# Pooled attention into a gated feed-forward layer on one core: sums spread over the gaps, two value blocks in gaps of their own, six buffers for normalised blocks

## Chip, cores, metric

One NeuronCore of a Trainium2 chip. The metric is the device time of one execution in microseconds (us). A run also reports its span (first to last instruction, usually some 2 us less than the time) and the mean granted TensorE clock (1.0 is full speed). Executions over 1.5% above the fastest of their kernel are marked slow, and the ratios below leave them out.

## The reference, cut to what matters

```python
# attention: q, k, v are (8 batches, 8 heads, 576 rows, 64)
k_p = k.reshape(B, H, 72, 8, D).mean(axis=3)        # keys pooled by 8
v_p = v.reshape(B, H, 72, 8, D).mean(axis=3)        # values pooled by 8
attn = softmax(q @ k_p.T / sqrt(D)) @ v_p
x = attn.transpose(0, 2, 1, 3).reshape(4608, 512)
# feed-forward: w_gate, w_val (512, 1536), w_out (1536, 512)
out = (maximum(x @ w_gate, 0) * (x @ w_val)) @ w_out
```

## The kernel before

Tokens are worked in nine chunks of 512, numbered from 0. In chunk c TensorE (PE) does twelve *pairs* (gate and value matmuls of 128 columns of the hidden layer, eight matmuls of 512 columns) and, from chunk 2 on, seven *products* of the chunk before. A product replaces part of the output matmul by a Strassen-like scheme, which needs four *sums* of blocks of h. VectorE (DVE) forms them, each in two halves, so a chunk has eight half sums; where a run speaks of a "sum", it is one of these. Attention of batch c+1 is woven into chunk c: the key transposes, sixteen score matmul groups, and five value blocks.

```python
relu_pool = tile_pool(name="relup", bufs=3)
piece_pool = tile_pool(name="piecep", bufs=4)                # px: one normalised value block
ps_mm = tile_pool(name="ps_mm", bufs=4, space=PSUM)          # pairs, transposes
ps_at = tile_pool(name="ps_at", bufs=3, space=PSUM)          # scores, value blocks
ps_acc = tile_pool(name="ps_acc", bufs=1, space=PSUM)        # products
# ... cut ...
def values(b, t):                                            # one value block, cut
    x = piece_pool.tile([P, NG, 2, D], F16, name="px")
    for half in range(2):
        ps = ps_at.tile([P, 512], F32, name="at_ps", tag="at_ps")
        # four matmuls into ps, then on VectorE:
        nc.vector.reciprocal(out=rd[:n, half], in_=pv[:, :, D:D + 2])          # prd
        nc.vector.tensor_tensor(out=x[...], in0=pv..., in1=rd..., op=ALU.mult) # px
# back(b, t, nc.sync) then sends px through a transposing DMA into x_T
# ... cut ...
for c in range(1, n_chunks):
    # ... cut: units = pairs with products between them ...
    others, later = attention(c + 1)       # one list per gap: [keys], [], scores, values
    for i, piece in enumerate(left):       # two value blocks left over from batch 2
        others[1 + i].insert(0, piece)
    for i, unit in enumerate(units):
        if i == 3: prep(c + 2, ...)        # GpSimd pools keys and values, starts loads
        unit()
        if c == 1: run(sums[i:i + 1])
        elif i:    run(sums[2 * i - 2:2 * i])
        if i < len(others): run(others[i])
```

In the traces DVE works through its instructions in the order of this program, so the place of a sum in the loop is its place in DVE's queue. *px* is a value block after normalising (a reciprocal, *prd*, and a multiplication); until DVE has read a block out of its bank of `ps_at`, PE can't use that bank again.

The softmax here doesn't subtract the row's maximum and nothing guards it: scores larger than these inputs give would overflow.

## Time and profile before

| | value |
|---|---|
| time, three runs | 334.33, 334.46, 334.75 us |
| the execution that was profiled | 337.71 us, span 335.8, mean clock 0.990 |
| busy: PE, DVE, GpSimd (POOL), ScalarE (ACT) | 97%, 64%, 42%, 38% of the span |
| chain that ended last | PE 90%, DVE 5% |

In the profile's rows of slices a digit is the busy share (or the clock) in tenths. In a chain row the columns are start, length, engine and line. In a timeline row a bracket at the end names how long the engine stood before the instruction, and for what.

### The profile page before, as it was taken

The page shows a single profiled execution, that of the slowest core. Times are in us where ns is not written, and L with a number is a line of the kernel's source. Part 1 is how long each engine was busy: PE and PEld are TensorE (multiplying, and loading weights), DVE is VectorE, ACT ScalarE, POOL GpSimd, SP SyncE. Part 2 cuts the span into 40 slices and gives each one's busy share as a digit, 9 for nine tenths or more (in the row PEclk, how much of TensorE's full clock was granted, in tenths as well). Part 3 has the DMA queues.
Part 4 walks back from the last instruction along what each step waited for, and adds up shares of the span by engine and source line. Part 5 has one row for each costly group of instructions (what it writes and reads, how often), then busy time and mean ns, then how long its engine had stood idle before and what let it go on. Part 6 is the DMA issues. An engine that isn't in the chain of part 4 may idle for free.

```text
span 335.8 us, 6528 instructions
## 1 busy us (share of the span) xinstructions
PE 325.3 (97%) x2526; PEld 214.2 (64%) x2526; DVE 214.7 (64%) x456; ACT 128.7 (38%) x295; POOL 139.8 (42%) x186
## 2 busy tenths in 40 slices
PE   8899999999969999999999999999999999999995
PEld 2578875455536665766898966655666556566574
DVE  7465637768666757785777667766576464464562
ACT  1544562473426224722471247124822332232231
POOL 8557419999999801993099309300000000000000
PEclk9999999999969999999999999999999999999999
DMA  7999998998559246963984462243022300300224
GB/s 112 190 204 201 200 214 159 188 153 171 106 101 185 47 90 94 205 101 74 159 158 79 81 107 58 33 64 104 1 24 56 113 5 0 98 29 3 65 75 110
DMA packets 51006, 35.41 MB, mean 105 GB/s; under 512 B 30432, under 2 KB 45024, under 8 KB 50976
## 3 DMA queue, kind: packets, MB, share of 16 engines
q0 software_dynamic: 18304, 18.88, 34.3%
q1 hardware_dynamic: 32528, 16.00, 24.0%
q8 instruction: 19, 0.31, 0.4%
q10 hardware_dynamic: 144, 0.13, 0.1%
q14 instruction: 11, 0.09, 0.1%
HBM read 37.75 MB, written 9.44 MB: 141 GB/s over the span
## 4 chain that ended last, share of the span: by engine, by line
PE 90%; DVE 5%; DMA 2%; ACT 1%; issue 1%; POOL 1%; DVEq 0%; ACTq 0%; POOLq 0%
PE mm_ps L429 54%; PE acc_ps L521 19%; PE at_ps L310 5%; PE mm_ps L467 3%; PE at_ps L388 3%; PE mm_ps L594 2%; DMA q<-in_q_dram 2%; DVE px L394 1%; DVE h L438 1%; PE mm_ps L411 1%; DVE sum L512 1%; PE mm_ps L281 1%; PE mm_ps L341 1%; PE mm_ps L365 1%; ACT pexp L370 1%
## 5 line engine op out<-in xcount | busy, mean ns | idle before, releaser
L438 DVE TENSOR_TENSOR h<-mm_ps,relu 128x512 f16<-128x512 f32 (+1 forms) x120 | 76.4, 637 | 87.6 <-PE mm_ps L429 79.8
L435 ACT ACTIVATE relu<-mm_ps 128x512 f16<-128x512 f32 (+1 forms) x120 | 66.5, 554 | 137.4 <-PE mm_ps L429 135.3
L429 PE MATMUL mm_ps<-x_T,wv_sb 128*128 128x512 f16 (+1 forms) x528 | 114.0, 342 | 0.1
L429 PE MATMUL mm_ps<-x_T,wg_sb 128*128 128x512 f16 (+1 forms) x528 | 114.0, 342 | 0.0
L429 PEld LDWEIGHTS <-wv_sb 128*128 128x128 f16 x528 | 51.7, 98 | 42.9 <-issue 1.1
L429 PEld LDWEIGHTS <-wg_sb 128*128 128x128 f16 x528 | 48.7, 98 | 28.9 <-issue 1.4
L324 ACT ACTIVATE expT<-at_ps 72x288 f16<-72x288 f32 (+2 forms) x128 | 39.1, 374 | 19.0 <-PE at_ps L310 18.9
L521 PEld LDWEIGHTS <-sum 128*128 128x128 f16 x336 | 32.1, 98 | 7.2
L394 DVE TENSOR_TENSOR px<-at_ps,prd 128x256 f16<-128x256 f32 (+1 forms) x80 | 33.8, 423 | 2.7
L181 POOL TENSOR_TENSOR tree_b<-tree_a 72x256 f32<-72x256 f32 (+1 forms) x42 | 32.0, 763 | 3.3
L521 PE MATMUL acc_ps<-wo_sums,sum 128*128 128x256 f16 x252 | 31.0, 272 | 0.0
L175 POOL TENSOR_TENSOR tree_a<-v_in 72x512 f32<-72x512 f16 x24 | 29.9, 1244 | 0.1
L521 PEld LDWEIGHTS <-h 128*128 128x128 f16 x252 | 23.9, 99 | 4.1
L175 POOL TENSOR_TENSOR tree_a<-k_in 96x512 f32<-96x512 f16 x18 | 20.7, 1149 | 11.5 <-DMA k_in<-in_k_dram 11.5
L521 PE MATMUL acc_ps<-wo_sb,h 128*128 128x256 f16 x168 | 21.1, 276 | 0.0
L529 DVE TENSOR_TENSOR rows<-acc_ps,mid 128x512 f32<-128x512 f32 x21 | 14.5, 689 | 8.8 <-PE acc_ps L521 8.8
L680 POOL COPY gate<-h 128x1 f16<-128x1 f16 x4 | 1.9, 463 | 43.4 <-DVE h L438 43.4
L512 DVE TENSOR_TENSOR sum<-h 128x768 f16<-128x768 f16 x28 | 19.8, 746 | 0.1
L388 PEld LDWEIGHTS <-expT 72*128 72x128 f16 (+1 forms) x280 | 13.0, 100 | 7.5 <-DVE px L394 1.6
L393 DVE RECIPROCAL prd<-at_ps 128x4 f32<-128x4 f32 (+1 forms) x80 | 13.7, 172 | 4.0 <-PE at_ps L388 3.9
L388 PE MATMUL at_ps<-stat,expT 72*128 72x65 f16 (+1 forms) x280 | 14.8, 194 | 1.4 <-DVE px L394 1.4
L186 POOL TENSOR_TENSOR stat<-tree_b 72x128 f16<-72x128 f32 x24 | 12.1, 506 | 1.9
(106 smaller groups left out, 300.2 us busy)
## 6 DMA issues: line engine op xcount, KB each, us to landing
out_dram<-rows SPq DMA_DIRECT2D x24, 256.0 KB
k_in<-in_k_dram POOLq DMA_DIRECT2D x7, 576.0 KB, 8.0
q<-in_q_dram POOLq DMA_DIRECT2D x7, 576.0 KB, 9.9
v_in<-in_v_dram POOLq DMA_DIRECT2D x6, 576.0 KB, 13.5
wg_sb<-in_moe_w_gate_dram POOLq DMA_DIRECT2D x6, 256.0 KB, 10.9
wv_sb<-in_moe_w_val_dram POOLq DMA_DIRECT2D x6, 256.0 KB, 10.8
wo_sb<-in_moe_w_out_dram POOLq DMA_DIRECT2D x3, 512.0 KB, 9.6
v_in<-in_v_dram POOLq DMA_DIRECT2D x2, 512.0 KB, 11.3
```

What stands on the lines that cost most here:

```text
L175: eng.tensor_tensor(out=cell["a"][:n], in0=src[:, :, :4 * D], in1=src[:, :, 4 * D:], op=ALU.add)
L181: eng.tensor_tensor(out=cell["c"][:n], in0=a[:n, :, :2 * D], in1=a[:n, :, 2 * D:], op=ALU.add)
L310: nc.tensor.matmul(out=ps[:SP, c0:c0 + cnt * QP], lhsT=kpTs[b % 2][j][:, h, :], rhs=queries(b, h, i0, cnt), start=True, stop=True,)
L324: nc.scalar.activation(out=out_ap, in_=in_ap, func=AF.Exp, scale=EXP_SCALE)
L388: nc.tensor.matmul(out=ps[:n, c0:c0 + D + 1], lhsT=weights(b, h, t), rhs=stats[b % 2][:SP, g, s0:s0 + D + 1], start=True, stop=True,)
L394: nc.vector.tensor_tensor(out=x[:n, half * NG // 2:(half + 1) * NG // 2, :, :], in0=pv.rearrange("p g (x c) -> p g x c", x=2)[:, :, :, :D] ...
L429: nc.tensor.matmul(out=t[:, lo:hi], lhsT=w[:, ci, fsl], rhs=x_T[:, ci, x0:x0 + hi - lo], start=(ci == 0), stop=(ci == n_co - 1),)
L435: nc.scalar.activation(out=relu[:, :n], in_=ps[0][:, :n], func=AF.Relu)
L438: nc.vector.tensor_tensor(out=h_tiles[c][:, fo, t0:t0 + n], in0=ps[1][:, :n], in1=relu[:, :n], op=ALU.mult)
L512: nc.vector.tensor_tensor(out=S[k][:, i], in0=x[:, i], in1=y[:, i], op=op)
L521: nc.tensor.matmul(out=ps[:, tb, :], lhsT=lhs[:, i, tb * P:(tb + 1) * P], rhs=rhs[:, i, :], start=(first and tb == 0 and i == 0), stop=(tb ...
L529: nc.vector.tensor_tensor(out=out_ap, in0=x, in1=y, op=ALU.add)
```

## The change

The intent was to shorten DVE's queue at the start of a chunk, where PE waits for px, by putting one sum in each gap, and to give transposes more slack with six px buffers.

```diff
-    piece_pool = ctx.enter_context(tc.tile_pool(name="piecep", bufs=4))
+    piece_pool = ctx.enter_context(tc.tile_pool(name="piecep", bufs=6))
 ... cut: prep is split in prep_k and prep_v, both still called at unit 3 ...
+        SUMS_AT = [1, 2, 3, 4, 5, 6, 13, 14]
 ...
-                for i, piece in enumerate(left):
-                    others[1 + i].insert(0, piece)
+                if left:
+                    others[1:2] = [[piece] for piece in left]
 ...
-                elif i:
-                    run(sums[2 * i - 2:2 * i])
+                elif c == n_chunks - 1:
+                    run(sums[max(2 * i - 2, 0):2 * i])
+                elif i in SUMS_AT:
+                    sums[SUMS_AT.index(i)]()
```

## The prediction

> **What bounds the kernel now.** I read the page first. Its first part gives PE 325.3 us busy, 97% of the span, against DVE 64%, and its fourth part puts 90% of the chain that ended last on PE. So a change can only pay where PE is not fed, and the second part, in 40 slices of 8.4 us, says where that is:
>
> ```profile
> PE   8899999999969999999999999999999999999995
> ...
> PEclk9999999999969999999999999999999999999999
> ```
>
> There is one hole, slice 11 (92.3 to 100.7 us), and the granted clock falls in the same slice. To see whether anything else is left in the later chunks I took the whole chain in order of time (columns: start us, length us, engine and line, count). A chunk is 512 tokens; its twelve gate-and-value pairs are eight 512-column matmuls each (L429), 1.73 us, and three such pairs run in a row where a chunk ends and the next begins, which marks a period:
>
> ```profile
> 85.36 3.47 PE mm_ps L429 x16
> ...
> 124.10 5.18 PE mm_ps L429 x24
> ...
> 157.87 5.20 PE mm_ps L429 x32
> ...
> 225.66 5.18 PE mm_ps L429 x24
> ...
> 259.43 5.18 PE mm_ps L429 x24
> ```
>
> From 225.66 to 259.43 is 33.77 us. Its content: 12 pairs x 1.73 = 20.8, 7 output products x 1.31 = 9.2, so 30.0; the remaining 3.8 is attention work, matmuls too (24 for scores, 40 for values, 7 transposes). The next period, which has no attention, runs from 259.43 to 289.32 in the same view: 29.9 us, the sum of pairs and products to 0.1. In five windows from 131 to 299 us PE is busy for the whole of each at clock 1.00. **Chunks 3 to 7 have next to nothing to give.** Chunk 2 is different: the row at 85.36 is one pair of chunk 1 and the first of chunk 2; the same place a chunk later is 124.10 + 1.73 = 125.83. That is 40.47 us. Chunk 2 does two value blocks more than a usual chunk, 16 small matmuls; eight take 0.25 us of PE (next pair starts 0.25 after them), so 0.5. Expected 34.3, taken 40.5: **an excess of about 6.2 us**.
>
> The chain between 84 and 104 us shows what it is made of:
>
> ```profile
> 88.92 0.69 DVE h L438
> 89.61 0.66 DVE kpT1l L264
> 90.27 0.01 issue
> 90.28 0.76 DVE kpT1u L264
> 91.04 0.01 issue
> 91.06 2.31 DVE sum L512 x2
> ...
> 93.61 0.42 DVE px L394
> ...
> 96.74 3.41 PE mm_ps L429 x8
> ```
>
> DVE has become the bound for 5.7 us: two copies of pooled keys, then two sums (2.31 us together), and only then the normalising of a value block (prd, px) that frees the attention PSUM banks (three of them). PE's own timeline shows the price:
>
> ```profile
> 92.33 0.32 PE L388 MATMUL at_ps<-stat,expT 72*64 72x65 f16 x4
> 94.09 0.32 PE L388 MATMUL at_ps<-stat,expT 72*64 72x65 f16 x4 [1.45 <-DVE px L394]
> 94.64 0.31 PE L310 MATMUL at_ps<-qT,kpT1l 128*72 128x288 f16 x1 [0.23 <-DVE px L394]
> 95.45 0.40 PE L310 MATMUL at_ps<-qT,kpT1u 128*72 128x256 f16 x2 [0.49 <-ACT expT L324]
> 96.34 0.40 PE L310 MATMUL at_ps<-qT,kpT1l 128*72 128x288 f16 x1 [0.49 <-ACT expT L324]
> ```
>
> The printed ends are modelled some 0.17 us late; by the spacing of such matmuls elsewhere (4 value matmuls 0.13, a score 0.13) PE really stands for about 1.6 + 0.4 + 0.7 + 0.6 = 3.3 us. Then the clock: by stretches of 2 us it is 1.00 to 94, 0.72, 0.50, 0.50, 0.57, 1.00, which places the half clock from 94.9 to 101.7. The pair at 96.74 takes 3.41 in place of 1.73 (1.7 lost), the five score matmuls after it 0.75 for some 0.35, the next product 1.76 for 1.31: 2.5 us. Idle 3.3 + cold 2.5 = 5.8, against 6.2 from the periods. The account closes within 0.4.
>
> **The Trainium skill.** "TensorE: Matmul & The Clock Gate", Part 1, says that the array drops to half clock after a window of about 3.4 us that is not busy, and returns after a busy one. The trace agrees: 6.8 us at 0.50, two such windows. The page does not say how idle a window must be; here one with PE shown busy 1.73 of 3.41 us (91.47 to 94.88) went cold, while one at 6.14 to 9.56 with 2.62 stayed warm. "SBUF — State Buffer", Who interferes with whom, says that a DVE instruction with two SBUF inputs contends with a GpSimd instruction that reads SBUF (it says so without a figure for this pair). The sums are such: undisturbed 0.55 us (minimum 548 ns, two in 1.03 us at 165.38), but 1.15 each at 91.06, where POOL's tree_a runs beside them.
>
> **The change, part by part.** A chunk's work is laid out in 18 units (a pair or a product each); behind each unit lies a gap for attention groups and sums. (1) Chunks 2 to 7 put one sum (half of one of four) behind each of units 1 to 6, and the last two behind units 13 and 14, where two stood behind each of units 1 to 4. Same 56 instructions, none added. (2) In chunk 2 the two value blocks left over from batch 2 get gaps of their own; they push all later attention groups of that chunk one unit back, so the three scores after the second block now come behind the next pair rather than in front of it. (3) Six px buffers in place of four. (4) Splitting the pooling routine in two moves nothing: both halves are called at unit 3, and the instruction order of POOL's work stays.
>
> Working through chunk 2 with measured durations. DVE: key copies end 91.04 as before; one sum, contended, to 92.2; the four normalising instructions, shifted 1.17 us earlier, free the first bank at 92.88 and the second at 93.43. PE: pair to 92.24, first half of the second block to 92.38; its second half waits for 92.94: idle 0.5. The pair that now follows runs 93.08 to 94.81, needing nothing from DVE but copies done at 91.04. First score to 94.93. Meanwhile DVE: h 93.4 to 94.0, second sum (contended) to 95.1, block two's px at 95.75 and 96.3. The second score waits to 95.81 (idle 0.9), the third to 96.35 (idle 0.4). After that product, exps and banks are in time. **Idle 1.8 in place of 3.3; 1.5 won. If the clock stays up, another 2.5 won: 4.0.** The account left 0.4 unplaced; I give back 0.1 of it. So 334.46 - 4.1 = 330.4 us.
>
> At the other end: sums 7 and 8 now lie behind the values, before product three, which reads them at unit 16. In chunk 2, counted from unit 9 with 1.17 us of DVE per block and 0.61 for h or an add, the last sum ends 12.4 us in, and PE wants its half at 12.1 + 0.33 = 12.4: just in time. In chunk 3, rows of before (product three starts at 156.56, DVE add at 154.87) put the last sum near 156.5, in time if POOL is idle there, some 0.4 late if not. Over all six chunks 0 to 1 us lost, 0.2 expected. The px buffers: none of DVE's listed waits is for a transpose out of a px buffer, so six for four is worth 0 by itself; it gives slack only.
>
> **Rivals.** *The clock falls all the same*: 1.8 us of idle in 4 us remain, a window of 3.4 us in the worst place would be near 60% busy, between the cold and the warm window above. Then one full window at half clock costs 1.7: 332.2. For it: the window is unfavourable if it starts near 93; against: the gap is broken by a whole pair. I give it 0.3. *A new wait takes the place of the old one*: the late sums hold up product three in every chunk, 0.5 x 6 = 3 us, leaving 331.5 to 333.5. For it: slack is near zero; against: POOL is done by then in most chunks, and DVE's own timeline shows gaps of 0.2 to 1.1 us at that place of chunk 2 (119 to 126 us). Chance 0.15. *Nothing is won, since PE is 97% busy*: against it stands the excess of 6.2 us in one place. *More is won*: all 6.2 at most, 328.3; even that is 1.8%, so over 2% is nearly shut out.
>
> **Range and chances.** 0.3 x 1.8 for the clock and 0.2 for the late sums would move the mean to 331.1; the likeliest case is 330.4. I set 330.7, range 329.2 to 332.8. Faster by over 2% (under 327.8) 0.03, within 2% 0.95, slower by over 2% 0.02.
>
> **What would show it.** In the changed profile: slice 11 of PE at 8 or 9 and PEclk 9 there; in PE's timeline at 92 to 97 us three waits of 0.5, 0.9 and 0.4 for px rather than 1.45 and after; period from the first pair of chunk 2 to that of chunk 3 near 36.4 us; later periods still 33.8; first sum alone of 1.15 us before the first px. It would be wrong if a clock drop is seen in another place, if PE waits for DVE sum at L521 in the later chunks, or if a px waits for a transpose.

## The result

Six runs of the changed kernel took 333.20 to 334.41 us, median 334.14; six of the kernel before had a median of 334.78. The ratio is 0.9971 (95% interval 0.9948 to 0.9993). A ratio is the mean time of one kernel's fast runs over that of the other's of the same rounds, so not quite the ratio of the medians. So the change saves about 1 us, where 3.8 were forecast, and the time lies above the range, though within 2%, to which the prediction gave 0.95.

The slices of the changed kernel:

```profile
PE   7899999999989999999999999999999999999994
...
PEclk9999999999999999999999999999999999999999
```

Hole and half clock are gone, as hoped. The chain, for the periods:

```profile
85.74 3.45 PE mm_ps L429 x16
...
120.28 5.18 PE mm_ps L429 x24
...
154.05 5.20 PE mm_ps L429 x32
...
221.84 5.18 PE mm_ps L429 x24
...
255.61 5.18 PE mm_ps L429 x24
```

From the first pair of chunk 2 to that of chunk 3 it is 120.28 + 1.73 - 85.74 = 36.27 us, against the 36.4 that the prediction named. Later periods stay at 33.77. PE's timeline in that place:

```profile
93.49 0.31 PE L388 MATMUL at_ps<-stat,expT 72*64 72x65 f16 x4 [0.47 <-DVE px L394]
93.74 1.04 PE L429 MATMUL mm_ps<-x_T,wg_sb 128*128 128x512 f16 x4
...
95.99 0.32 PE L310 MATMUL at_ps<-qT,kpT1u 128*72 128x256 f16 x2 [0.23 <-DVE px L394]
96.53 0.31 PE L310 MATMUL at_ps<-qT,kpT1l 128*72 128x288 f16 x1 [0.22 <-DVE px L394]
```

Three stands of 0.47, 0.23 and 0.22 as printed (each some 0.17 longer by the starts, so about 0.6, 0.4 and 0.4), with the pair between the first and the second. The order and the places are those of the working; the second stand is less than half of its 0.9. Ahead of the first one DVE has one half sum now, longer than the 1.15 us forecast:

```profile
91.43 1.33 DVE L512 TENSOR_TENSOR sum<-h 128x768 f16<-128x768 f16 x1
```

Against the profile of before, the span fell from 335.8 to 332.4, by 3.4 us. **The two profiles show the gain that was forecast; the times don't.** Before against before, 337.71 against 334.46, is where the two part.

### The profile page after: what moved, and what is told of

Its sections match the earlier page's. It is cut to its first block, busy times and chain, and to the rows that moved or that the text cites. A ratio compares the mean times of both kernels' runs of the same rounds, so it can differ in the third digit from the quotient of the medians.

```text
span 332.4 us, 6528 instructions
## 1 busy us (share of the span) xinstructions
PE 322.3 (97%) x2526; PEld 212.5 (64%) x2526; DVE 210.5 (63%) x456; ACT 128.7 (39%) x295; POOL 138.8 (42%) x186
## 3 DMA queue, kind: packets, MB, share of 16 engines
q0 software_dynamic: 18304, 18.88, 34.9%
## 4 chain that ended last, share of the span: by engine, by line
PE 91%; DVE 4%; DMA 2%; issue 1%; ACT 1%; POOL 1%; DVEq 0%; ACTq 0%; POOLq 0%
PE mm_ps L429 54%; PE acc_ps L521 19%; PE at_ps L310 4%; PE mm_ps L467 3%; PE at_ps L388 3%; PE mm_ps L594 2%; DMA q<-in_q_dram 2%; DVE px L394 2%; DVE h L438 1%; PE mm_ps L411 1%; PE mm_ps L281 1%; PE mm_ps L341 1%; PE mm_ps L365 1%; ACT pexp L370 1%; DVE prd L393 0%
## 5 line engine op out<-in xcount | busy, mean ns | idle before, releaser
L175 POOL TENSOR_TENSOR tree_a<-v_in 72x512 f32<-72x512 f16 x24 | 29.2, 1218 | 0.1
L512 DVE TENSOR_TENSOR sum<-h 128x768 f16<-128x768 f16 x28 | 17.7, 637 | 0.1
```

Of the source, the lines that this page charges most:

```text
L175: eng.tensor_tensor(out=cell["a"][:n], in0=src[:, :, :4 * D], in1=src[:, :, 4 * D:], op=ALU.add)
L512: nc.vector.tensor_tensor(out=S[k][:, i], in0=x[:, i], in1=y[:, i], op=op)
```

## The experiments

Every chunk-2 length below is worked out as above, from two rows of that run's chain, in the one execution that was profiled. The three profiles of the changed kernel differ there by 0.6 us among themselves, so smaller differences between single profiles say little. Medians of spans leave out executions of 338 us and more. The runs came in three calls, each on another chip: first the two kernels again, the sums alone and the layout alone; then more standing, six buffers alone, three buffers and the key copy; then the rest. Each is compared with the kernel before in its own call.

### The two kernels again

Theory A: the profile of before caught an exception. Rival B: the kernel before always falls to half clock in chunk 2.

> The kernel before, unchanged. Its profiled run took 337.71 us with a mean clock of 0.990, while its three timed runs took 334.33 to 334.75. Theory A (the half-clock stretch of 6.8 us in that profile was an exception, and the timed runs mostly have none): most runs here have spans of 332 to 333 us, mean clock 0.996 or more, times 334 to 335; a run with clock 0.990 is 2.5 to 3.3 us longer. A second profile shows full clock from 92 to 102 us. Rival B (the kernel before always falls to half clock there, and the profiled run was long for another reason): every run here has a mean clock near 0.990 and the profile again shows half clock after 94 us.

> The changed kernel, unchanged, beside it. Theory A: 1.0 us (0.3%) faster than the kernel before where neither goes to half clock, clock 0.997 to 1.000, span 331 to 332.6. Rival B: the spans differ by about 3.4 us in all runs and the time by as much.

The kernel before: 335.29 us (ratio to the kernel before 1.0013, 0.9979 to 1.0046). Its clocks were 1.0 in three runs, 0.997 in one, 0.995 in two. The new profile (its lines are numbered one less, as a blank line was cut), the chain, then PE's timeline, then DVE's:

```profile
85.98 3.45 PE mm_ps L428 x16
...
121.04 5.18 PE mm_ps L428 x24
```

```profile
93.76 0.31 PE L387 MATMUL at_ps<-stat,expT 72*64 72x65 f16 x4 [0.49 <-DVE px L393]
94.31 0.31 PE L309 MATMUL at_ps<-qT,kpT1l 128*72 128x288 f16 x1 [0.23 <-DVE px L393]
95.11 0.28 PE L309 MATMUL at_ps<-qT,kpT1u 128*72 128x256 f16 x2 [0.49 <-ACT expT L323]
95.89 0.28 PE L309 MATMUL at_ps<-qT,kpT1l 128*72 128x288 f16 x1 [0.49 <-ACT expT L323]
```

```profile
91.68 1.35 DVE L511 TENSOR_TENSOR sum<-h 128x768 f16<-128x768 f16 x2
```

Chunk 2 takes 121.04 + 1.73 - 85.98 = 36.79 us here, not 40.47. The first stand is 0.49, not 1.45, because the same two sums took 1.35 us, not 2.31. And the clock stays at 1.00 throughout. The same program has both profiles; ahead of the two sums they differ in where GpSimd's work stood. In the first profile it began a tree_a (a step of pooling) at 90.80, 0.26 us ahead of the first sum; in this one its tree_b, begun at 91.16, was nearly done when the sum came at 91.68. From the first profile, then from this one:

```profile
90.80 1.15 POOL L175 TENSOR_TENSOR tree_a<-k_in 96x512 f32<-96x512 f16 x1
```

```profile
91.16 0.72 POOL L180 TENSOR_TENSOR tree_b<-tree_a 96x256 f32<-96x256 f32 x1
```

Where GpSimd is idle, later in this profile, such a pair takes 1.03 us (at 128.50). That fits the contention which the prediction names, but no run moved GpSimd's work by itself.

The changed kernel: 333.26 us, ratio 0.9964 (0.9929 to 0.9998), clocks 0.996 to 1.0, chunk 2 in 35.65 us.

Each execution is listed with its clock, so the kernel before can be sorted (the first result lists no clocks for it). Of 39 executions 18 ran at 0.996 or more (median span 332.35), 16 below it but under 338 us (334.1), and 5 took 338 us or more. Of 18 executions of the changed kernel 17 ran at 0.996 or more (331.9), one at 0.995 (334.7), none took 338. Theory A holds in its main point: the state of the profiled execution, 0.990, was not the common one (five of the 39 were at 0.992 or below). Rival B falls. But theory A's "mostly none" was wrong, since 21 of the 39 lost some clock, 15 of them at 0.995 and under 338 us.

### More standing, and standing filled

> The kernel before with the first two sums of chunk 2 computed twice (1.1 us of DVE more undisturbed, up to 2.3 beside POOL's work), ahead of the px on which PE waits. Theory A2 (the half clock comes when PE's stand there grows past what a window of 3.4 us tolerates, and it was near that edge in the first profile): the profile shows PE standing 1.5 to 2.9 us before the second half of the value block, half clock from some 95 to 102 us, mean clock 0.985 to 0.993 in most runs, time 4 to 6 us over the kernel before. Rival (the clock falls by chance, whatever PE does): mean clock 0.995 to 1.000 in most runs and only 1 to 2.3 us longer.

```diff
                 elif i:
+                    if c == 2 and i == 1:
+                        run(sums[:2])
                     run(sums[2 * i - 2:2 * i])
```

339.37 us, ratio 1.0091 (1.0047 to 1.0135). All six executions lost clock, four at 0.990 and two at 0.995. PE's timeline:

```profile
95.60 0.32 PE L388 MATMUL at_ps<-stat,expT 72*64 72x65 f16 x4 [2.90 <-DVE px L394]
```

Chunk 2 took 41.90 us. More standing brings the half clock every time; the rival of pure chance falls. The loss is less than the 4 to 6 us expected, 3.1 by the ratio, as five of the eleven executions of the kernel before beside it had lost clock too.

> The kernel before with eight idle matmuls of 512 columns (0.22 us each, results unused) put on PE where it stands in chunk 2: four before the second half of the second block, two ahead of each of the last two scores of the group behind it. DVE's work is unchanged. Theory A2 (the stand brings the half clock): all clocks 0.997 or more, no span over 333.3, where about a third of the kernel before's are at 0.995 or less and 333.2 to 335.8; in undisturbed executions 0 to 0.6 us longer than the kernel before. Rival (the clock falls whatever PE does): a third of the executions at 0.995 or less here as well.

```diff
+            if (b, t, half) == (2, 4, 0):
+                warm(4)                      # in values(), after the four matmuls
 ...
+                if c == 2:
+                    v4, s0, s1, s2 = others[2]
+                    others[2] = [v4, s0, lambda: warm(2), s1, lambda: warm(2), s2]
```

Four of six executions were at 0.998 to 1.0 with spans 332.0 to 332.6, where 8 of 11 of the kernel before beside it were at 0.995 or less. The other two took 342.23 and 351.65 us; one of them is the profiled one, and its loss lies in chunk 1, ahead of the fillers:

```profile
72.23 0.28 PE L310 MATMUL at_ps<-qT,kpT0l 128*72 128x288 f16 x1 [3.81 <-DMA qT<-q]
```

A transposing DMA of queries was 15.4 us in flight there. In chunk 2 of that profile the clock is 1.00 and the length 36.89 us, that of an undisturbed chunk 2 of before. So filling costs and wins nothing at full clock, and in four of six executions no half clock came. The one of 351.65 us has no profile, so where it lost its clock is not known. The theory's "all clocks 0.997 or more" failed on these two; this supports theory A2 without settling it.

### The three parts one by one

> The kernel before with six px buffers, nothing else. The layout-only run with four buffers showed a px waiting 3.8 us for a transpose out of the buffer it needs, and 2 of its 6 executions took 340.7 and 343.7 us; the kernel before had 3 of 11 at 340.3 to 346.6. Theory C (late transposes behind four buffers make those executions): fast runs as before, 334 to 335 us, and no execution over 338 us here, while the kernel before beside it has some. Rival D (the long executions come from elsewhere, say the clock alone): one or two of six over 338 us here too. The blind working said that the buffers are worth 0 in every run.

335.15 us, ratio 0.9974 (0.993 to 1.0017): no difference. One of six took 349.34 us, and none of the eleven of the kernel before beside it took 338, so theory C, that four buffers make the long executions, falls. Its profile fell on an execution at 0.995. The stretches of 2 us (busy of five engines, then clock, DMA share, GB/s):

```profile
94.00:96.00 2.00, 1.02 (x6) 0.61 (x6) 1.97 (x6) 1.22 (x3) 1.92 (x3) 0.96 0.34 66
96.00:98.00 2.00, 2.00 (x6) 0.70 (x5) 0.46 (x2) 0.60 (x1) 1.84 (x5) 0.50 1.05 195
98.00:100.00 2.00, 2.00 (x15) 1.52 (x14) 1.36 (x3) 1.00 (x3) 1.98 (x4) 0.69 1.01 146
```

Half clock for some 3.4 us, one window, and chunk 2 in 38.42 us: 1.6 over the undisturbed 36.79. PE's stands were 0.47, 0.23, 0.49 and 0.49, the same as in the undisturbed profile to 0.02. So with this much standing the clock sometimes falls and sometimes doesn't.

> Only the sums are spread; the two left-over value blocks stay as in the kernel before (the second one in the gap of the first three scores), four px buffers. Theory A: the first px of the stretch comes some 1.2 us earlier, but the second sum and px still stand before the scores, with no pair between: PE still stands for 2 to 3 us, gain 0.4 to 0.8 us over the kernel before. If the spread alone is what the change is worth: about 1.0 us. If the layout alone is: 0.

333.77 us, ratio 0.9972 (0.9944 to 1.0001), median span 331.55, clocks 0.997 to 1.0, chunk 2 in 36.05 us. In the profile PE no longer stands before the second half block, and 0.17, 0.49 and 0.49 us before the scores, less than the 2 to 3 expected. By this profile spreading the sums alone is worth 0.7 us in chunk 2.

> Only the two left-over value blocks get gaps of their own; sums two to a gap in units 1 to 4 as before, four px buffers. Theory A: the wait for the first px stays 1.5 us, then a whole pair runs before the scores and covers some of the second wait: gain 0.2 to 0.6 us. If the layout alone is what the change is worth: about 1.0 us.

334.36 us, ratio 0.9971 (0.9934 to 1.0008), chunk 2 in 35.83 us: the layout alone is worth 1.0 us there, more than expected. The two parts add up to 1.7 us, more than the whole (0.5 to 1.2), and with one profile each they can't be ranked. Two of six took 340.69 and 343.68 us. The profiled execution has, in DVE's timeline of chunk 3:

```profile
151.17 0.42 DVE L394 TENSOR_TENSOR px<-at_ps,prd 64x256 f16<-64x256 f32 x1 [3.77 <-DMA x_T<-px]
```

A px waits for its buffer, as a transpose is 9.7 us in flight. This is the wait that six buffers were meant to remove, so they were put in here:

> Layout of the two left-over blocks plus six px buffers, sums as before. Theory C (long executions of the layout-only run came from px waiting for late transposes behind four buffers): no execution over 338 us and no px wait for a transpose in the profile; fast executions as in the layout-only run, spans 331.4 to 331.8. Rival D (long executions are independent of the buffers): again one or two of six over 338.

334.22 us, ratio 0.9957 (0.99 to 1.0013), chunk 2 in 35.82 us. One execution took 338.2 us, so theory C's "no execution over 338" missed here too. No px waits for a transpose any more, but in the profiled execution a transpose was late again (16.2 us on the chain), and PE's timeline shows the wait one step on:

```profile
160.00 0.61 PE L429 MATMUL mm_ps<-x_T,wg_sb 128*128 128x256 f16 x4 [2.30 <-DMA x_T<-px]
```

The next pair needs the transposed block itself. Here the wait is PE's and not DVE's; six buffers don't make the transpose land. Whether they would have hidden the flight of 9.7 us in the run before, no run shows.

> The changed kernel with three px buffers in place of six. Theory C: a px then waits for the transpose three blocks back, so waits for transposes appear in the profile in most chunks, and long executions are the rule: median 336 us or more, several over 338. Rival D: as the changed kernel, 333 to 334.5 us, no wait for a transpose.

334.67 us, ratio 0.9946 (0.9903 to 0.999), two of six at 340.3 us. The profiled one of these has one px wait for a transpose, of 4.93 us. So with three buffers a late transpose hurts, but four of six executions took 333.3 to 334.7 us, as the changed kernel does: theory C's "in most chunks" and "336 us or more" were wrong, and so was the rival's "none".

### Taking away what is left

> The changed kernel, with the upper copy of pooled keys of batch 3 on ScalarE in place of VectorE (0.76 us off DVE just before the stand), and the sums of chunk 2 moved: one behind unit 1, none behind unit 2, the last two behind unit 8. If what is left of the stand in chunk 2 (1.1 to 2.0 us over the 34.3 us that the later chunks lead one to expect) is DVE work ahead of px: chunk 2 in 34.3 to 34.9 us, 0.8 to 1.3 us faster than the changed kernel, 1.8 to 2.3 faster than the kernel before. If ScalarE becomes the wait: no gain over the changed kernel.

```diff
-        k_evacuate(b, ps, True, nc.vector)
+        k_evacuate(b, ps, True, nc.scalar if b == 3 else nc.vector)
 ...
+        SUMS_2 = {1: (0,), 3: (1,), 4: (2,), 5: (3,), 6: (4,), 7: (5,), 8: (6, 7)}   # chunk 2
```

333.41 us, ratio 0.9928 (0.9892 to 0.9965), the lowest of all. All six executions ran at 0.997 or more, with a median span of 330.95. Chunk 2 took 35.28 us, not 34.3 to 34.9: the waits for px are gone, and a product now waits for the fourth half sum:

```profile
99.56 1.16 PE L521 MATMUL acc_ps<-wo_sums,sum 128*128 128x256 f16 x9 [0.60 <-DVE sum L512]
```

The last step moved that sum forward, and the changed kernel was run beside it:

> The changed kernel once more, beside the runs of this call. Theory A (what remains of the gain is 0.4 to 1.1 us of stand in chunk 2, plus a half-clock window of 3.4 us, worth 1.7 us, that a third of the executions of the kernel before have and this one does not): ratio 0.995 to 0.998, all clocks 0.996 or more, spans 330.8 to 333.0.

> The kernel with the key copy on ScalarE, with all sums ahead of the values: in chunk 2 one behind unit 1, two behind unit 3, one each behind 4, 5 and 6, two behind 7; in later chunks one each behind units 1 to 6 and two behind 7. Its predecessor still lost 1.1 us in chunk 2 (a product waiting for the fourth sum) and 0.4 us in chunk 3 (a product waiting for the last sum, 0.93 and 1.25 us long beside POOL). Expected: chunk 2 in 34.3 to 34.7 us, chunk 3 in 33.8, span 329.2 to 330.2, 1.2 to 2.2 us under the changed kernel. If sums in front of the values only move the wait to the first value blocks: no gain over its predecessor (span 330.6 to 331).

The changed kernel: 334.25 us, ratio 0.9961 (0.9909 to 1.0014), chunk 2 in 35.64. One execution was at 0.995, against theory A's "all at 0.996 or more". The new version: chunk 2 in 34.50 us, as expected, but 335.38 us, ratio 0.9955 (0.9897 to 1.0014), no better. The profile shows a late transpose again, 15.8 us on the chain, with a wait of 2.07 us at a pair. Two of the six spans are 330.7 and 331.1; the others are 333.0 to 336.3. The same stretch of 2 us in this kernel, then in the changed kernel beside it:

```profile
134.00:136.00 2.00, 2.00 (x15) 1.24 (x14) 1.72 (x3) 1.28 (x4) 1.84 (x4) 1.00 1.09 24
```

```profile
134.00:136.00 2.00, 2.00 (x22) 1.79 (x20) 1.97 (x3) 1.20 (x4) 1.92 (x3) 1.00 1.07 218
```

In both the DMA engines are shown busy throughout (1.09 and 1.07); they move 24 GB/s in one and 218 in the other. What SyncE, which issues the transposes, does some us later in the two:

```profile
140.81 15.12 SPq L407 DMA_TRANSPOSE x_T<-px  x5
```

```profile
141.53 8.22 SPq L406 DMA_TRANSPOSE x_T<-px  x5
```

The same is in five profiles: layout only (four px buffers), layout with six, three buffers, key copy on ScalarE, and this one. In these the DMAs move 22 to 33 GB/s from 134 to 136 us, the five transposes take SyncE 10.1 to 15.5 us from the first issue to the end of the last, and GpSimd waits for a load of keys as well, for 0.2 to 9.6 us. It is in none of the three profiles of the changed kernel and the two of the kernel before, where SyncE takes 8.2 us. So ordinary loads are late with the transposes, and three, four and six buffers all have it. Why, no run tells, and with one profile each, whether an order makes it likelier is open too.

## Why the prediction was right or wrong

- **That chunks 3 to 7 have next to nothing to give.** Right: periods of 33.77 us before and after in undisturbed executions.
- **The changed chunk 2.** Right in its path: 36.4 us forecast, 36.27, 35.65 and 35.64 measured. The waits came in the order and the places given, with the first half sum alone (1.33 us) ahead of px. That the number fits so closely is in part luck: the stands were about 1.4 us in place of 1.8, and a product waits 0.3 for the last sum. None of the three signs of being wrong that the prediction named came in the profile of the changed kernel.
- **"Expected 34.3, taken 40.5: an excess of about 6.2 us".** This is the step that failed: the length of chunk 2 before. The 40.47 us is that of the profiled execution; an undisturbed one takes 36.79, an excess of 2.5. The prediction took a saving measured from a 337.71 us execution off a median of 334.46, so 3.25 us were counted that the median did not contain.
- **"If the clock stays up, another 2.5 won".** The mechanism is supported (more standing brought half clock in six of six), but the term was mis-sized. With half clock for two windows of 3.4 us, the profile was beyond the common case. 21 of 39 executions of before lost clock; the 16 below 338 us are 1.75 us longer at the median, what one such window costs. Of the changed kernel one execution of 18 lost clock.
- **"1.5 won" for the standing.** Mis-sized too: in chunk 2, 36.79 against 35.6 to 36.3 gives 0.5 to 1.2 us. The 3.3 us of standing held a contended pair of sums (2.31 us) that another execution does in 1.35. There PE stands for about 2.4 us (1.70 as printed, and 0.17 more for each of the four), against 1.4 in the changed kernel.
- **The account of what was won.** At full clock the median spans differ by 332.35 - 331.9 = 0.45 us. The lost clock adds 16/39 x 1.75 - 1/18 x 2.8 = 0.6 us. Together about 1.0, which is what the first ratio says (0.29% of 334.8). This is an estimate: it mixes executions of several chips. That the lost clock lies in chunk 2 is shown for the two executions whose profiles caught it there (the first one, and six buffers alone).
- **Late sums, 0.2 us.** Right: in the changed kernel one product in chunk 2 takes 1.61 us in place of 1.31, and the third products of later chunks take 1.31.
- **Six buffers worth 0.** Right for the time. With a late transpose, DVE waits for a px buffer in two traces with three and four buffers, and PE for the block itself in two with six; how often six help is open.
- **The rivals.** The one of a clock that falls all the same was asked of the changed kernel only. It should have been asked of the profile of before.

What sends an execution with the same four stands (0.47 to 0.49 us three times, 0.23 once) into half clock or not, and what makes transposes late, stays open. The prediction's thought that it depends on where the window starts is untested.

## What to carry to other kernels

Compare the time of the profiled execution with the median before you take an account from its profile, and take the saving off the time of that same execution. If they differ by as much as the gain you forecast, take a second profile first. Judge a small change by a length inside the trace, such as the chunk in question, taken from more than one profile of each kernel, and by the list of executions sorted by clock, for the median mixes the two states.

## What the Trainium skill lacked or had wrong

- "TensorE: Matmul & The Clock Gate", Why this matters for your kernels, advises no PE-idle gaps over about 3 us between bursts. In the first profile here the longest printed gap in that place was 1.45 us and the clock fell for 6.8 us; with four gaps of 0.23 to 0.49 us it fell for some 3.4 in one execution and not in another. Short gaps close together count. The page has a case of this too (A second HAM failure mode: psum-queue depth-cycling, where short idles between groups of matmuls make the clock go up and down), but gives neither a length of the gaps nor a share of a window.
- "SBUF — State Buffer", Who interferes with whom, has the contention of a two-input VectorE instruction with GpSimd's reads, but no size for this pair. Here one sum takes 548 ns undisturbed and up to 1,948 beside GpSimd, and the same pair of sums 1.35 or 2.31 us in two executions of one program.
- "DMA: Bandwidth & Descriptors", Rules for kernel authors, says of a transpose next to ordinary DMAs that it "needs nothing", which there is a matter of correct results. The runs show no wrong result, but flights of 9.0 to 16.2 us on the chain in some executions, in one of them after a stretch in which the DMA engines were busy and moved 24 GB/s. The page has no figure for such a flight.
